# The gates of the last two token chunks by seven block products in place of eight, with sums made in PSUM banks

## The chip, the cores and the metric

The kernel runs on one core of one Trainium2 chip. The metric is the device time of one execution in microseconds. Five engines work side by side, each through its own instructions in order, and wait for each other by semaphores: TensorE (PE) multiplies matrices into PSUM, VectorE (DVE) and ScalarE (ACT) read PSUM and SBUF, GpSimd (POOL) works on SBUF, and SyncE (SP) issues most DMAs. PSUM has eight banks of 512 f32 columns here; SBUF is the working memory.

## The reference

```
phi(x) = elu(x) + 1                       # q, k, v: [8 batches, 8 heads, 576, 64]
kv = phi(k).T @ v ;  z = sum(phi(k))      # per batch and head
x  = (phi(q) @ kv) / (phi(q) . z + 1e-6)  # -> [4608 tokens, 512]
a  = x @ w1 ;  b = x @ w2                 # [4608, 1024] each
out = ((a * b) @ w3) @ w_out              # [4608, 512]
```

Inputs and output are f32. The two last products are one with the weight wf = w3 @ w_out.

## The kernel before

The 4608 tokens are 36 tiles of 128, and four tiles make one of nine chunks c0 of 512 columns. Attention gives x for three tiles at a time (NT makes numerators and denominators on PE, NM divides on VectorE), and a DMA transposes it (XD) into `xt` of a chunk: 512 features in four blocks of 128 rows, bf16.

The feed-forward part of a chunk has two kinds of steps. `F.c0.f` (f from 0 to 7) makes 128 of the 1024 hidden features for the chunk's 512 tokens: four matmuls for side a (`a_ps`), four for side b (`b_ps`), each into a PSUM bank of its own; ScalarE copies a to SBUF (L492), and VectorE multiplies the copy with b into the bf16 tile `ab` (L494). `O.t` makes the output of one tile t: eight matmuls with `wf_sb` into one bank (L536), a copy by ScalarE (.a) or VectorE (.v) (L543), and `S.t` stores it in two DMAs. `Q.35` is the last tile, in three pieces.

Other steps that the change moves: L (loads: LV is v), EX, PT and PM (phi of q or k: exp on ScalarE, two operations on VectorE), VC (v to bf16), KB (kv of a batch), QD (transposed q by DMA).

A table of text, `ORDER`, lists all steps; the program is emitted in that order, and each engine gets its instructions in it. PSUM is given out by hand: four single banks (kind "mm") and two tiles of two banks (kind "at"), first freed first taken. SBUF buffers of the loads (kind "ld", 13 of them) are handed out in the same way. A tile framework puts in the semaphore waits.

Of the kernel before, what the change touches and what calls it, by code (L numbers as in the profile page):

```python
# [19 lines left out]
T3.7.0.v LO.0 CO.0.a LO.2 CO.1.v FW.2.0.a T3.7.1.a LO.3 FW.4.0.a CO.3.a LQ.0.0 L3.6 FW.7.0.a
PT.q.0.0 L3.1 FW.2.1.a FW.4.1.a EX.q.0.0 LQ.0.1 PM.q.0.0 CO.2.p FW.2.2.a FW.7.1.a FW.7.2.v FW.7.3.a
FW.4.2.a FW.4.3.v QP.0.0.v C3.6.a LK.0.0 T3.1.0.a T3.1.1.a PT.q.0.1 FW.2.3.v L3.3 L3.5 T3.6.0.v
T3.6.1.v EX.q.0.1 LK.0.1 FW.1.0.a FW.1.1.a PT.k.0.0 FW.1.2.a PM.q.0.1 FW.6.0.a FW.6.1.v FW.6.2.v
LH.0.0 EX.k.0.0 T3.3.0.a T3.3.1.a FW.1.3.a C3.5.v T3.5.0.a FW.6.3.v EX.k.0.1 PT.k.0.1 LV.0.0 LV.0.1
LH.0.1 FW.3.0.a FW.3.1.v T3.5.1.a FW.3.2.v FW.3.3.v PM.k.0.1 LA.0 LB.6 I.2 CA.0.p CB.6.p LB.7
PM.k.0.0 T3.0.0.a LA.1 FW.5.0.a VC.0.0.a QP.0.1.v FW.0.0.a FW.0.1.a KV.0.0.a LA.2 VC.0.1.v FW.5.1.v
T3.0.1.v KV.0.1.a NT.0 NM.0.0 NM.0.1 CB.7.p FW.0.2.a FW.0.3.a NM.0.2 FW.5.2.a FW.5.3.a LA.3 XP.0.a  # L30
CA.2.p XP.1.v ND.3 LB.2 CA.1.v XP.2.a LB.3 FS.0.0.0.0 FS.0.1.0.0 FS.0.1.1.0 FS.0.0.1.0 LQ.1.1 LK.1.0
XP.3.v FS.0.2.0.0 FS.0.2.1.0 FS.0.2.0.1 FS.0.2.1.1 CB.2.v FS.0.0.0.1 FS.0.0.1.1 FS.0.1.0.1
FS.0.1.1.1 FS.0.3.0.1 CB.3.v PT.q.1.1 CA.3.p F.0.4 EX.q.1.1 PM.q.1.1 PT.k.1.0 LQ.1.0 LV.1.0 PT.q.1.0
EX.k.1.0 FS.0.3.0.0 LK.1.1 F.0.5 F.0.6 PM.k.1.0 VC.1.0.v EX.q.1.0 PM.q.1.0 QP.1.1.a EX.k.1.1
FS.0.3.1.0 PT.k.1.1 LV.1.1 F.0.7 KV.1.0.a LQ.2.1 LQ.3.1 VC.1.1.a QP.1.0.a O.0.a PM.k.1.1 KV.1.1.v
LV.2.0 FS.0.3.1.1 EX.q.3.1 NT.4 NM.4.0 NM.4.1 O.1.a NM.4.2 EX.q.2.1 PT.q.2.1 LK.2.0 XP.4.a ND.7
XP.5.a LK.2.1 EX.k.2.1 LK.3.1 O.2.a PT.q.3.1 PT.k.2.1 LV.3.0 XP.6.v XP.7.v LV.2.1 EX.k.2.0 PM.k.2.1
LV.3.1 O.3.a PT.k.2.0 LQ.2.0 S.0.s LQ.3.0 PM.k.2.0 PM.q.2.1 VC.2.0.v LV.4.1 F.1.0 F.1.1 PT.k.3.1
# [24 lines left out]

# [1 line left out]
def kernel(  # L65
# [473 lines left out]

    def s_O(t, e):  # L540
        o_ps = o_mm(t, slice(0, DM))
        o_sbs[t] = take("o_sb", None, [P, DM], F32, "o_sb")
        copy_of(e)(out=o_sbs[t], in_=o_ps)  # L543
        give("mm", "o_ps")

    def store(queues, t, o_sb, cols):
        for g in range(2):
            b, j = divmod(2 * t + g, J)
            queues[g].dma_start(out=out[b * S:(b + 1) * S, :].rearrange("(p j) n -> p j n", j=J)[:, j, cols],
                                in_=o_sb[g * R:(g + 1) * R, cols])  # L550
# [53 lines left out]
```

## Time and profile before

| | us |
|---|---|
| median of three runs | 240.89 (240.65 to 241.69) |
| span of the profiled execution, first to last instruction | 239.7 |
| PE busy | 233.2 |
| DVE busy | 151.0 |
| ACT busy | 115.0 |
| POOL busy | 8.1 |

The page gives the span of the profiled execution and no time of its own beside it. Busy times are sums over an engine's instructions; an engine that is busy for less than the span may still be waited for at some place. Rows of the timeline give the start, the duration, the engine, the line of the kernel, what is written and read, and in brackets the idle time before and what ended it. Matmuls overlap at their ends, so a row of four shows 1.03 us where the next four start 0.86 us later.

### The profile page before, as it was taken

How to read it: one execution, taken by the hardware profiler on the slowest of the kernel's cores; microseconds unless marked ns; L12 is line 12 of the kernel's file. 1: busy time of each engine (PE TensorE's matmuls, PEld its weight loads, DVE VectorE, ACT ScalarE, POOL GpSimd, SP SyncE). 2: the span in 40 equal slices, each digit the busy share in tenths (PEclk: the TensorE clock that was granted, in tenths of full speed). 3: DMA queues.
4: the chain of work that ended last, by engine and by line, in shares of the span. 5: the costliest groups of instructions: out<-in, count | busy, mean ns of one | idle time of the engine just before them, and what ended most of it. 6: DMA issues, size and time to landing. Idle time of an engine off the chain costs nothing.

```text
span 239.7 us, 5540 instructions
## 1 busy us (share of the span) xinstructions
PE 233.2 (97%) x2276; PEld 120.2 (50%) x2276; DVE 151.0 (63%) x278; ACT 115.0 (48%) x173; POOL 8.1 (3%) x15
## 2 busy tenths in 40 slices
PE   8899999999999999999999999999999999999994
PEld 5656668555445444444454444545444444444443
DVE  0347787889999646877862588885546363433341
ACT  2576743979793255568522656424232113321300
POOL 1020053000000000000000000000000000000000
PEclk9999999999999999999999999999999999999999
DMA  6999999999996999999879959965293763005216
GB/s 241 402 406 397 379 375 390 390 390 389 396 332 137 158 357 247 323 406 296 190 106 192 392 123 262 320 116 131 52 178 69 174 157 88 3 0 125 50 24 154
DMA packets 52553, 55.81 MB, mean 233 GB/s; under 512 B 31280, under 2 KB 32560, under 8 KB 52528
## 3 DMA queue, kind: packets, MB, share of 16 engines
q1 hardware_dynamic: 52288, 55.19, 78.5%
q8 instruction: 18, 0.29, 0.5%
q10 hardware_dynamic: 240, 0.26, 0.3%
q14 instruction: 7, 0.06, 0.1%
HBM read 38.80 MB, written 9.44 MB: 201 GB/s over the span
## 4 chain that ended last, share of the span: by engine, by line
PE 96%; DVE 1%; ACT 1%; issue 0%
PE o_ps L536 26%; PE a_ps L483 25%; PE b_ps L483 24%; PE wf_ps L264 6%; PE nd L399 3%; PE w3p L252 3%; PE warm L149 2%; PE kbp L341 2%; PE a_ps L516 2%; PE b_ps L516 2%; PE xp L458 1%; PE qp L369 1%; PE kvp L341 1%; ACT wo_sb L218 0%; ACT w3b L238 0%; DVE w3t L253 0%
## 5 line engine op out<-in xcount | busy, mean ns | idle before, releaser
L483 PEld LDWEIGHTS <-w_sb 128*128 128x128 bf16 x544 | 52.6, 98 | 62.5 <-DVE xt L459 0.3
L494 DVE TENSOR_TENSOR ab<-a_sb,b_ps 128x512 bf16<-128x512 f32 x68 | 46.2, 686 | 39.9 <-PE b_ps L483 38.6
L492 ACT COPY a_sb<-a_ps 128x512 f32<-128x512 f32 x68 | 39.8, 586 | 64.0 <-PE a_ps L483 63.6
L483 PE MATMUL a_ps<-xt,w_sb 128*128 128x512 bf16 x272 | 69.9, 380 | 0.0
L483 PE MATMUL b_ps<-xt,w_sb 128*128 128x512 bf16 x272 | 69.8, 379 | 0.0
L536 PE MATMUL o_ps<-wf_sb,ab 128*128 128x512 bf16 (+2 forms) x304 | 65.2, 368 | 0.0
L536 PEld LDWEIGHTS <-ab 128*128 128x128 bf16 x304 | 28.4, 98 | 31.7 <-issue 0.4
L543 ACT COPY o_sb<-o_ps 128x512 f32<-128x512 f32 x22 | 12.9, 586 | 33.5 <-PE o_ps L536 26.7
L405 DVE TENSOR_TENSOR xn<-nd,r 128x512 bf16<-128x512 f32 (+2 forms) x47 | 23.8, 559 | 0.3
L274 ACT ACTIVATE ek<-k 128x1152 bf16<-128x1152 f32 x16 | 18.7, 1172 | 0.7 <-ACT ek L274 0.7
L274 ACT ACTIVATE eq<-q 128x1152 bf16<-128x1152 f32 x16 | 18.7, 1168 | 0.4 <-DMA q<-in_q_dram 0.4
L543 DVE COPY o_sb<-o_ps 128x512 f32<-128x512 f32 x13 | 9.0, 691 | 15.3 <-PE o_ps L536 12.6
L264 PE MATMUL wf_ps<-wo_sb,w3t 128*128 128x512 bf16 x64 | 15.6, 380 | 0.5 <-ACT wo_sb L218 0.5
L286 DVE TENSOR_SCALAR phq<-q 128x1152 bf16<-128x1152 f32 x16 | 12.0, 755 | 2.7 <-DMA q<-in_q_dram 2.7
L294 DVE TENSOR_TENSOR phk<-phk,ek 128x1152 bf16<-128x1152 bf16 x16 | 11.9, 750 | 1.8 <-ACT ek L274 1.7
L294 DVE TENSOR_TENSOR phq<-phq,eq 128x1152 bf16<-128x1152 bf16 x16 | 12.1, 755 | 1.0 <-ACT eq L274 0.8
L286 DVE TENSOR_SCALAR phk<-k 128x1152 bf16<-128x1152 f32 x16 | 12.0, 753 | 0.0
L264 PEld LDWEIGHTS <-w3t 128*128 128x128 bf16 x64 | 5.9, 98 | 5.8 <-issue 0.7
L328 ACT CAST vt<-v 128x1152 bf16<-128x1152 f32 x7 | 8.1, 1162 | 0.9 <-DMA v<-in_v_dram 0.9
L253 ACT CAST w3t<-w3p 128x512 bf16<-128x512 f32 x7 | 4.0, 587 | 9.3 <-PE w3p L252 7.4
L399 PEld LDWEIGHTS <-qt 64*64 64x64 bf16 x576 | 6.1, 106 | 4.3 <-issue 4.1
L399 PE MATMUL nd<-kv,qt 64*64 64x65 bf16 x576 | 7.6, 194 | 0.4 <-DVE w3t L253 0.4
(57 smaller groups left out, 127.4 us busy)
## 6 DMA issues: line engine op xcount, KB each, us to landing
q<-in_q_dram SPq DMA_DIRECT2D x16, 576.0 KB, 8.3
k<-in_k_dram SPq DMA_DIRECT2D x16, 576.0 KB, 9.5
v<-in_v_dram SPq DMA_DIRECT2D x16, 576.0 KB, 10.5
out_dram<-o_sb SPq DMA_DIRECT2D x69, 128.0 KB, 2.5
w<-in_moe_w_dram SPq DMA_DIRECT2D x7, 512.0 KB, 10.9
wo<-in_moe_w_out_dram SPq DMA_DIRECT2D x4, 512.0 KB, 8.2
wa<-in_moe_w_dram SPq DMA_DIRECT2D x4, 512.0 KB, 10.7
wb<-in_moe_w_dram SPq DMA_DIRECT2D x4, 512.0 KB, 10.4
```

What stands on the lines that cost most here:

```text
L264: nc.tensor.matmul(wfs[i], w3ts[i][:, c, :], wo_sb[:, c, :], start=(c == 0), stop=(c == FC - 1))
L274: nc.scalar.activation(out=t, in_=raw[n, b, h], func=AF.Exp)
L286: (nc.gpsimd if e == "p" else nc.vector).tensor_scalar(out=by_set(n, t), in0=by_set("k", raw[n, b, h]), scalar1=0.0, scalar2=1.0, op0=ALU. ...
L294: nc.vector.tensor_tensor(out=t, in0=t, in1=by_set("k", es[n, b, h]), op=ALU.min)
L399: nc.tensor.matmul(dst[g * R:(g + 1) * R], qts[b, a // 2][rows, j, a % 2 * R:(a % 2 + 1) * R], kvs[b][rows, a // 2, a % 2, :], start=True, ...
L405: nc.vector.tensor_tensor(out=xn[:, :, a0:a1], in0=n4[:, :, :, 0:D], in1=r.unsqueeze(3).to_broadcast([P, 2, a1 - a0, D]), op=ALU.mult)
L483: nc.tensor.matmul(ops_[key][:, tiles.start * P:tiles.stop * P], w[:, w_row(kc), f * P:(f + 1) * P], xts[c0][:, tiles, kc, :], start=(kc = ...
L492: nc.scalar.copy(out=a_sbs[c0, f], in_=ops_[key])
L494: nc.vector.tensor_mul(out=abs_[c0][:, f, :], in0=a_sbs[c0, f], in1=ops_[key])
L516: nc.tensor.matmul(p, w[:, w_row(kc), f * P:(f + 1) * P], xts[c0][:, 2 * g:2 * g + 2, kc, :], start=(kc == 0), stop=(kc == KC - 1))
L536: nc.tensor.matmul(o_ps, abs_[c0][:, f, m * P:(m + 1) * P], wf_sb[:, f, cols], start=(f == 0), stop=(f == FC - 1))
L543: copy_of(e)(out=o_sbs[t], in_=o_ps)
```

## The change

For chunks 7 and 8 together, the gates are taken as a 2 by 2 block product: the hidden features in two halves, the 512 input features in two halves, the two chunks as two halves of the columns. Seven block products take the place of eight, for each of four values of f and each side (Winograd's form of Strassen's method). The weight sums (four for each side, step WS) are made on GpSimd, the sums of `xt` (four, step WT) on VectorE. A step `WP.7.f.side.i` makes product i in two matmuls of 512 columns, and takes the results apart in a row of sums: products 1, 6, 7, 4 build up in the first bank of an "at" tile, 5 and 3 in the second, 2 in an "mm" bank. ScalarE copies the bank after 1, 5 and 6 (and after 4 on side a); VectorE adds such a copy to the bank after 2, 7 and 3. On side b the sum is multiplied with side a's at once, in SBUF, into the bf16 tile `abq`.

```diff
+    def ws_of(side, i):
+        key = ("ws", side, (i - 1) // 2)
+        if key not in wsum:
+            wsum[key] = late(key, 4).rearrange("p (i r n) -> p i r n", i=2, r=2)
+        return wsum[key][:, (i - 1) % 2]
...
+    def s_WS(side, i, e):
+        w = (w1_sb, w2_sb)[side]
+        a, b, op = {1: (w_half(w, 0, 1), w_half(w, 1, 1), ALU.add),
+                    2: (ws_of(side, 1), w_half(w, 0, 0), ALU.subtract),
+                    3: (w_half(w, 0, 0), w_half(w, 0, 1), ALU.subtract),
+                    4: (w_half(w, 1, 0), ws_of(side, 2), ALU.subtract)}[i]
+        (nc.gpsimd if e == "p" else nc.vector).tensor_tensor(out=ws_of(side, i), in0=a, in1=b, op=op)
...
+    def w_mm(ps, c0, f, side, i, first):
...
+        for r in range(2):
+            nc.tensor.matmul(ps, lhs[:, r, f * P:(f + 1) * P], rhs[:, :, r, :],
+                             start=(first and r == 0), stop=(r == 1), skip_group_check=not first)
...
+    def w_add(c0, f, side, ps, tmp, c, g):
+
+        nc.vector.tensor_tensor(out=tmp, in0=ps, in1=tmp, op=ALU.add)
+        if side == 0:
+            wtmp[c0, f, "a", c, g] = tmp
+        else:
+            nc.vector.tensor_mul(out=w_ab(c0, f)[:, c, g], in0=wtmp.pop((c0, f, "a", c, g)), in1=tmp)
+
+    def s_WP(c0, f, side, i, e):
+        q = c0, f, side
+        if i in (1, 5) and q not in wbank:
+            wbank[q] = at_tile("wp" + "ab"[side], ("wp",) + q)
+        if i == 2:
+            wbank[q + ("x",)] = mm_tile("wx" + "ab"[side], ("wx",) + q)
+        ps = wbank[q + ("x",)] if i == 2 else wbank[q][:, 0 if i in (1, 6, 7, 4) else 1]
+        w_mm(ps, c0, f, side, i, i in (1, 2, 5))
+        if i in (1, 5, 6):
+            t = wtmp[q + (i,)] = w_tmp({1: "e", 5: "phq", 6: "phk"}[i], "p" + str(i) + "ab"[side])
+            nc.scalar.copy(out=t, in_=ps)
+        elif i == 2:
+            w_add(c0, f, side, ps, wtmp.pop(q + (1,)), 0, 0)
+            give("mm", ("wx",) + q)
+        elif i == 3:
+            w_add(c0, f, side, ps, wtmp.pop(q + (6,)), 1, 0)
+        elif i == 7:
+            w_add(c0, f, side, ps, wtmp.pop(q + (5,)), 1, 1)
+        elif side == 0:
+            t = wtmp[c0, f, "a", 0, 1] = w_tmp("w3t", "p4a")
+            nc.scalar.copy(out=t, in_=ps)
+        else:
+            nc.vector.tensor_mul(out=w_ab(c0, f)[:, 0, 1], in0=wtmp.pop((c0, f, "a", 0, 1)), in1=ps)
+        if i == 4:
+            give("at", ("wp",) + q)
```

The order is another one from the step behind `PM.q.6.1` on; ahead of it nothing is changed. A piece of the table as it was (all of F.7) and as it is:

```diff
-S.22.s S.23.s O.26.v O.27.v F.7.0 S.24.s XD.8.0 S.25.s F.7.1 F.7.2 F.7.3 F.7.4 F.7.5 F.7.6 XD.8.1
+WP.7.2.1.3 WP.7.2.1.4 O.27.a WP.7.3.0.5 S.26.s WP.7.3.0.1 S.20.s WP.7.3.0.2 WP.7.3.1.1 WP.7.3.1.2
```

Products and PE's other steps in their new order, a product written as f, side, number (0a1 is WP.7.0.0.1), and the first product some 22 us of PE work behind `PM.q.6.1`:

```
0a1 F.6.7 F.6.4 0b1 F.6.2 O.22 0a2 0a6 0a5 0b5 F.6.5 0a7 0a3 0b6 0b3 0a4 0b7 F.6.6 0b4
1a1 0b2 1a5 1a6 1b1 F.6.0 1a7 1b6 1a3 1b5 1a4 1b7 O.24 2b1 1b4 1b3 O.20
2a1 2b6 2b5 2a6 1a2 2a5 1b2 2a7 O.26 2b7 2a3 2a4 2a2 2b3 2b4 O.27
3a5 3a1 3a2 3b1 3b2 3a6 3b6 3b5 3a7 2b2 3b7 3a3 3a4 O.25 3b4 3b3
O.30 O.31 O.32 O.34 O.29 O.33 O.28 Q.35
```

The attention steps of the last batch (KB.7, NT.30, NT.33, QD.7, XD.7, XD.8) now all come ahead of 0a1.

Three places show how instructions stand on the engines. First TensorE, before, where one side's matmuls end and the next begin in an F step of chunk 8:

```order
L483 MATMUL b_ps<-xt,w_sb 128x512
L483 LDWEIGHTS w_sb
L483 MATMUL a_ps<-xt,w_sb 128x512 [waits Activation_49]
L483 LDWEIGHTS w_sb
L483 MATMUL a_ps<-xt,w_sb 128x512
```

TensorE in the changed kernel at 2a3, 2a4 and 2a2 (`wpa` is the tile of two banks of side a, `wxa` the single bank of product 2, `ws` and `xs` the sums):

```order
L632 LDWEIGHTS ws
L632 MATMUL wpa<-xt,ws 128x512 [waits DVE_49]
L632 LDWEIGHTS ws
L632 MATMUL wpa<-xt,ws 128x512
L632 LDWEIGHTS w_sb
L632 MATMUL wpa<-xs,w_sb 128x512 [waits DVE_49]
L632 LDWEIGHTS w_sb
L632 MATMUL wpa<-xs,w_sb 128x512
L632 LDWEIGHTS w_sb
L632 MATMUL wxa<-xt,w_sb 128x512
```

Before, a wait comes once in four matmuls and is for a bank used two steps earlier; now 2a4, into the first bank, waits for a VectorE instruction, and the count of its wait is that of the add behind 2a3, which reads the second bank. Second, VectorE, before, from the divisions of NT.33 to the multiplications of chunks 7 and 8:

```order
L405 TENSOR_TENSOR xn<-nd,r 128x512
L543 COPY o_sb<-o_ps 128x512 [waits DMAHW7_49,DMAHW0_49,PE_49]
L543 COPY o_sb<-o_ps 128x512 [waits DMAHW2_49,DMAHW1_49,PE_49]
L494 TENSOR_TENSOR ab<-a_sb,b_ps 128x512 [waits PE_49,Activation_49] x11
L543 COPY o_sb<-o_ps 128x512 [waits DMAHW4_49,DMAHW3_49,PE_49]
```

VectorE in the changed kernel, from the add behind 3a7 to the end of the products:

```order
L648 TENSOR_TENSOR p5a<-wpa,p5a 128x512 [waits PE_49]
L648 TENSOR_TENSOR p1b<-wxb,p1b 128x512 [waits PE_49]
L652 TENSOR_TENSOR abq<-p1a,p1b 128x512 [waits DVE_49]
L648 TENSOR_TENSOR p5b<-wpb,p5b 128x512 [waits PE_49,Activation_49]
L652 TENSOR_TENSOR abq<-p5a,p5b 128x512 [waits DVE_49]
L648 TENSOR_TENSOR p6a<-wpa,p6a 128x512 [waits PE_49]
L676 TENSOR_TENSOR abq<-p4a,wpb 128x512 [waits PE_49,Activation_49]
L648 TENSOR_TENSOR p6b<-wpb,p6b 128x512 [waits PE_49]
L652 TENSOR_TENSOR abq<-p6a,p6b 128x512 [waits DVE_49]
```

One multiplication for each F step has become a row of adds and multiplications, and the add behind 3a3 (`p6a`) stands fourth behind the add of 3a7 (`p5a`), after two adds and two multiplications for other products. Third, GpSimd, whose last instructions before were casts of weights in the front of the program:

```order
L227 CAST w_sb<-wb 128x2x512 [waits DMAHW4_49]
L227 CAST w_sb<-wb 128x2x512 [waits DMAHW5_49]
L222 CAST w_sb<-wa 128x2x512 [waits DMAHW7_49]
L222 CAST w_sb<-wa 128x2x512 [waits DMAHW0_49]
L599 UNCONDITIONAL_BRANCH
```

In the changed kernel, behind the same casts:

```order
L616 TENSOR_TENSOR ws<-w_sb 128x1024 [waits DMAHW1_49,DMAHW5_49,DVE_49,DMAHW6_49,Activation_49,Pool_49]
L616 TENSOR_TENSOR ws<-w_sb 128x1024 [waits DVE_49,DMAHW2_49,PE_49,DMAHW6_49,Activation_49,Pool_49]
L616 TENSOR_TENSOR ws<-ws,w_sb 128x1024 [waits Pool_49] x2
L616 TENSOR_TENSOR ws<-w_sb,ws 128x1024 [waits DMAHW2_49,DMAHW4_49,Activation_49,Pool_49]
L616 TENSOR_TENSOR ws<-w_sb,ws 128x1024 [waits DMAHW2_49,DMAHW7_49,DVE_49,Activation_49]
L616 TENSOR_TENSOR ws<-w_sb 128x1024 x2
```

Eight sums are added. They wait for the last readers of the load buffers that they write: VC.5.1 for the first, PT.k.7.0 for the second, VC.6.0 for the fifth and EX.k.7.1 for the sixth, all of them steps in the part that isn't changed.

More of the change, by code (lines that the diff above doesn't have):

```diff
@@ L16 @@
 NCH = 512
+PAIRS = (7,)
 ORDER = """
 L3.7 L3.4 L3.2 LO.1 I.0 H.1.1 H.3.0 H.1.2 I.1 T3.4.0.a H.2.3 T3.2.0.v T3.2.1.a T3.4.1.v H.1.4 C3.7.a
[L23 to L38, printed above, removed]
@@ L530, in s_FP, with ab_of @@
             f_out(c0, f, side)
+    def ab_of(c0, f):
+        if c0 in PAIRS:
+            return quads[c0, f % 4][:, 0, f // 4]
+        if c0 - 1 in PAIRS:
+            return quads[c0 - 1, f % 4][:, 1, f // 4]
+        return abs_[c0][:, f]
     def o_mm(t, cols):
@@ L535, in o_mm @@
         for f in range(FC):
-            nc.tensor.matmul(o_ps, abs_[c0][:, f, m * P:(m + 1) * P], wf_sb[:, f, cols],
+            nc.tensor.matmul(o_ps, ab_of(c0, f)[:, m * P:(m + 1) * P], wf_sb[:, f, cols],
                              start=(f == 0), stop=(f == FC - 1))
@@ L544, in s_O @@
         give("mm", "o_ps")
+        c0 = t // CT - (t // CT - 1 in PAIRS)
+        if c0 in PAIRS:
+            n = uses["o", c0] = uses.get(("o", c0), 0) + 1
+            if n == 2 * CT:
+                for f in range(FC // 2):
+                    give("ld", ("abq", c0, f))
     def store(queues, t, o_sb, cols):
@@ L563, in s_Q, with late, w_half, x_half @@
             store((nc.sync, nc.scalar), t, o_sb, slice(pieces[0][0], pieces[-1][1]))
+    quads, wsum, xsum, wbank, wtmp, uses = {}, {}, {}, {}, {}, {}
+    def late(key, n):
+        t = take("ld", key, [P, HW], F32, key[0]).bitcast(BF16)[:, 0:n * NCH]
+        return t
+    def w_half(w, k, fh):
+        return w[:, 2 * k:2 * k + 2, fh * NCH:(fh + 1) * NCH]
+    def x_half(c0, k):
+        return xts[c0][:, :, k::2, :]
+    def ws_of(side, i):
[3 more added lines that the diff above has]
+        return wsum[key][:, (i - 1) % 2]
@@ new lines, in xs_of @@
+    def xs_of(c0, i):
+        key = ("xs", c0, (i - 1) // 2)
+        if key not in xsum:
+            xsum[key] = late(key, 4).rearrange("p (i m r n) -> p i m r n", i=2, m=CT, r=2)
+        return xsum[key][:, (i - 1) % 2]
+    def s_WS(side, i, e):
[5 more added lines that the diff above has]
+        (nc.gpsimd if e == "p" else nc.vector).tensor_tensor(out=ws_of(side, i), in0=a, in1=b, op=op)
@@ new lines, in s_WT @@
+    def s_WT(c0, i, e):
+        b11, b12, b21, b22 = x_half(c0, 0), x_half(c0 + 1, 0), x_half(c0, 1), x_half(c0 + 1, 1)
+        a, b = {1: (b12, b11), 2: (b22, xs_of(c0, 1)), 3: (b22, b12), 4: (b21, xs_of(c0, 2))}[i]
+        (nc.gpsimd if e == "p" else nc.vector).tensor_tensor(out=xs_of(c0, i), in0=a, in1=b, op=ALU.subtract)
+    def w_mm(ps, c0, f, side, i, first):
+        w = (w1_sb, w2_sb)[side]
+        lhs = {1: lambda: w_half(w, 0, 0), 2: lambda: w_half(w, 1, 0), 3: lambda: ws_of(side, 4),
+               4: lambda: w_half(w, 1, 1), 5: lambda: ws_of(side, 1), 6: lambda: ws_of(side, 2),
+               7: lambda: ws_of(side, 3)}[i]()
+        rhs = {1: lambda: x_half(c0, 0), 2: lambda: x_half(c0, 1), 3: lambda: x_half(c0 + 1, 1),
+               4: lambda: xs_of(c0, 4), 5: lambda: xs_of(c0, 1), 6: lambda: xs_of(c0, 2),
+               7: lambda: xs_of(c0, 3)}[i]()
+        for r in range(2):
+            nc.tensor.matmul(ps, lhs[:, r, f * P:(f + 1) * P], rhs[:, :, r, :],
+                             start=(first and r == 0), stop=(r == 1), skip_group_check=not first)
@@ new lines, in w_tmp, with w_ab @@
+    def w_tmp(kind, name):
+        t = take(kind, None, [P, FC, P] if kind == "w3t" else [P, HW], BF16, name)
+        if kind == "w3t":
+            t = t.rearrange("p c t -> p (c t)")
+        return t.bitcast(F32)[:, 0:NCH]
+    def w_ab(c0, f):
+        if (c0, f) not in quads:
+            quads[c0, f] = late(("abq", c0, f), 4).rearrange("p (c g n) -> p c g n", c=2, g=2)
+        return quads[c0, f]
+    def w_add(c0, f, side, ps, tmp, c, g):
[4 more added lines that the diff above has]
+            nc.vector.tensor_mul(out=w_ab(c0, f)[:, c, g], in0=wtmp.pop((c0, f, "a", c, g)), in1=tmp)
@@ new lines, in s_WP @@
+    def s_WP(c0, f, side, i, e):
[23 more added lines that the diff above has]
+            give("at", ("wp",) + q)
+        if i > 3:
+            n = uses[c0, i in (4, 7)] = uses.get((c0, i in (4, 7)), 0) + 1
+            if n == 4 * FC // 2:
+                give("ld", ("xs", c0, int(i in (4, 7))))
+        if i in (3, 5, 6, 7):
+            n = uses["s", side, i in (3, 7)] = uses.get(("s", side, i in (3, 7)), 0) + 1
+            if n == FC * len(PAIRS):
+                give("ld", ("ws", side, int(i in (3, 7))))
```

63 lines of the change are left out of this document (42 added, 21 removed).

## Prediction

> **What bounds the kernel now.** I read the shares of the page first, then the chain that ended last, then a table by stretches of time, then the rows of the last chunks one by one.
>
> ```profile
> span 239.7 us, 5540 instructions
> PE 96%; DVE 1%; ACT 1%; issue 0%
> ```
>
> ```profile
> core 0: us, PE busy (x) PEld busy (x) DVE busy (x) ACT busy (x) POOL busy (x), PEclk, DMA share, GB/s
> 0.00:20.00 20.00, 17.42 (x90) 11.74 (x91) 6.86 (x11) 10.12 (x13) 2.72 (x10) 1.00 0.92 355
> 150.93:173.50 22.57, 22.57 (x334) 11.29 (x332) 15.88 (x32) 8.31 (x13) 0.00 (x0) 1.00 0.65 142
> 173.50:218.50 45.00, 45.00 (x301) 20.55 (x300) 21.51 (x39) 11.79 (x21) 0.00 (x0) 1.00 0.44 96
> ```
>
> TensorE (PE) holds 96% of the chain, and in the stretches that the change rewrites (the last two rows) it is busy for all of the time at a granted clock of 1.00, while VectorE (DVE) and ScalarE (ACT) are less than three quarters busy. So a matmul taken out here shortens the kernel by its full slot, as long as nothing new makes PE wait. The slot comes from the chain in order of time:
>
> ```profile
> 227.47 0.86 PE a_ps L483 x4
> 228.33 0.86 PE b_ps L483 x4
> ```
>
> Four 128x512 matmuls hold the chain for 0.864 us (228.33 less 227.47 is 0.86), so one is 0.216 us and a product of two matmuls 0.43 us.
>
> **What is removed.** Chunks 7 and 8 took 16 steps of 8 matmuls, 128 in all. Now they take 4 output blocks f, 2 sides, 7 products, 2 matmuls each: 112. That is 16 x 0.216 = **3.5 us less** on PE.
>
> **What is added on PE: waits.** A product is called f, side, number here: 2a4 is product 4 of side a in block f = 2. The products of one f and side share one PSUM tile of two banks (only number 2 has a bank of its own). By design 1, 6, 7, 4 build up in the first bank and 5, 3 in the second, and the order of products makes use of that: 7 and 3, or 6 and 5, often follow each other directly. But the waits in the built program are by the tile and not by the bank: the first matmul of 2a4 waits for VectorE's read of 2a3, and the wait count it names is that of the add issued just for 2a3, although that add reads the other bank. So PE has to stand through a whole read. What a read takes, from a matmul's last slot to the next start:
>
> ```profile
> 225.58 1.03 PE L483 MATMUL a_ps<-xt,w_sb 128*128 128x512 bf16 x4
> 226.44 1.03 PE L483 MATMUL b_ps<-xt,w_sb 128*128 128x512 bf16 x4
> 226.65 0.58 ACT L492 COPY a_sb<-a_ps 128x512 f32<-128x512 f32 x1 [1.14 <-PE a_ps L483]
> 227.31 1.03 PE L483 MATMUL a_ps<-xt,w_sb 128*128 128x512 bf16 x4
> 227.58 0.69 DVE L494 TENSOR_TENSOR ab<-a_sb,b_ps 128x512 bf16<-128x512 f32 x1 [1.04 <-PE b_ps L483]
> ...
> 10.57 1.05 ACT L218 CAST wo_sb<-wo 128x1024 bf16<-128x1024 f32 x1
> 11.67 0.59 PE L264 MATMUL wf_ps<-wo_sb,w3t 128*128 128x512 bf16 x2 [0.54 <-ACT wo_sb L218]
> ```
>
> The a group's slots end at 226.44, and ScalarE starts at 226.65: 0.21 us for the end of the pipeline and the semaphore. Its copy takes 0.58. PE starts 0.05 us after the engine it waits for (11.67 less 11.62). So a wait on ScalarE costs 0.21 + 0.58 + 0.05 = **0.84 us**, less what PE has to do in between. VectorE starts 0.27 after the slots (227.58 less 227.31) and takes 0.69: **1.01 us**. The adds themselves (PSUM plus an SBUF tile, f32) are not in the trace; L494, with the same operands and a bf16 result, is the nearest row; bounds are the 0.42 us of the same operation at half the width and the 0.755 of a product of two SBUF tiles of over twice the width:
>
> ```profile
> L494 DVE TENSOR_TENSOR ab<-a_sb,b_ps 128x512 bf16<-128x512 f32 x68 | 46.2, 686 | 39.9 <-PE b_ps L483 38.6 <-ACT a_sb L492 0.8 <-issue 0.3
> L294 DVE TENSOR_TENSOR phq<-phq,eq 128x1152 bf16<-128x1152 bf16 x16 | 12.1, 755 | 1.0 <-ACT eq L274 0.8
> L523 DVE TENSOR_TENSOR ab<-a_sb,b_ps 128x256 bf16<-128x256 f32 x8 | 3.3, 420 | 1.6 <-PE b_ps L516 1.5
> ```
>
> I take 0.69 for sums and multiplications.
>
> Going down the order of products, 19 of them stand directly behind a read of their own tile, or one or two products behind it, and these are all the waits that are not covered:
> - ScalarE, nothing in between: 0a5, 0b3, 1a6, 2b5, 3a1, 3b5: 6 x 0.84 = 5.0
> - ScalarE, one product (0.43) in between: 1a5, 2a5, 2a7: 3 x 0.41 = 1.2
> - VectorE, nothing in between: 0a3, 1b3, 2a4, 2b4, 3a4, 3b3: 6 x 1.01 = 6.1
> - VectorE, one in between: 0b7, 1a3, 1a4: 3 x 0.58 = 1.7; two in between: 3a3, 0.15
>
> That makes 18 waits with a cost and one of 0.15, **14.2 us**. All others have an F or O step of 1.73 us, or two products, ahead of them and cost nothing.
>
> Where VectorE has a queue, the wait is longer, since it works in order. Two operations back to back take 1.28 us, so one behind another starts 0.60 later; a product of two sums has to wait for the second sum, and starts 0.03 after its end, as here (182.12, then 182.15):
>
> ```profile
> 140.37 1.28 DVE L494 TENSOR_TENSOR ab<-a_sb,b_ps 128x512 bf16<-128x512 f32 x2
> ...
> 181.95 0.17 DVE L432 TENSOR_SCALAR r<-nd 128x10 f32<-128x10 f32 x1
> 182.15 0.30 DVE L433 RECIPROCAL r<-r 128x24 f32<-128x24 f32 x1
> ```
>
> The worst is 3a4. Count from the end of 3a7's slots: VectorE adds for 3a7 at 0.27 to 0.96, for 2b2 at 0.88 to 1.57, multiplies at 1.60 to 2.29, adds for 3b7 at 2.21 to 2.90, multiplies at 2.93 to 3.62, and only then adds for 3a3, at 3.54 to 4.23. PE could have begun 3a4 at 1.44 and begins at 4.28: 2.84 in place of 1.01, **1.8 more**. In the same way 2a4 waits 1.91 (the add of 2b7 and a multiplication stand ahead): 0.9 more. 0a3, 1a3 and 2b4 find one operation ahead and lose 0.2 each, and four copies on ScalarE 0.05 to 0.08 each: 0.8 together. **The waits come to 14.2 + 3.5 = 17.7 us**, in a stage that holds 208 matmuls (112 of the products, 48 of six F steps, 48 of six O steps), 45 us of PE work.
>
> VectorE as a whole isn't the bound: 40 operations for 16, six F and two O steps and four sums of xt come to 52 x 0.69 = 36 us in a stage that is 45 us of PE work alone. ScalarE makes 28 copies for 16, 12 x 0.58 = 7 us more, with three quarters of the stretch idle now (11.79 of 45).
>
> **What is moved, and other new work.** Batch 7's divisions (NT.30, NT.33) come some 16 to 20 us sooner. Behind them VectorE has 10 us of work in the 11.7 us between F.5.2 and NT.27 and about as much up to the first product; the transposes XD of chunks 7 and 8 are issued about as their divisions end, and F.6.7 and F.6.4 (3.5 us) cover the sums that wait for them. I take 0; it would cost up to 0.8 if that cover falls short.
>
> The eight weight sums on GpSimd (POOL) wait only for buffers long free, so they start far ahead of their place in the order: the last four at 135.6, when ScalarE has cast a v tile, and run in a row.
>
> ```profile
> 33.17 1.04 POOL L227 CAST w_sb<-wb 128x1024 bf16<-128x1024 f32 x1 [0.34 <-DMA wb<-in_moe_w_dram]
> 35.59 0.68 DVE L222 CAST w_sb<-wa 128x1024 bf16<-128x1024 f32 x1
> 35.99 1.18 POOL L222 CAST w_sb<-wa 128x1024 bf16<-128x1024 f32 x1 [1.78 <-DMA wa<-in_moe_w_dram]
> ...
> 134.43 1.16 ACT L328 CAST vt<-v 128x1152 bf16<-128x1152 f32 x1
> 137.22 0.75 DVE L286 TENSOR_SCALAR phk<-k 128x1152 bf16<-128x1152 f32 x1
> 141.27 1.03 PE L483 MATMUL b_ps<-xt,w_sb 128*128 128x512 bf16 x4
> ```
>
> A GpSimd cast of 128x1024 takes 1.04 us alone and 1.18 when it starts under a VectorE cast. A sum reads two operands, so my estimate from these rows is 1.04 to 2.1 us. Nobody waits for the sums (the first product that needs one is 40 us later); the cost can only be VectorE held up by them. Its slack there: the product at 140.37 ends at 140.97 and frees the bank that PE writes from 141.27, so 0.3 us. Bounds 0 and 7 us (below); I take 0.4, nearest to the 0.14 that the row at 35.99 shows.
>
> At the end, the store of O.28 now stands ahead of the last tile's on the SP queue:
>
> ```profile
> 177.27 2.48 SPq L549 DMA_DIRECT2D out_dram<-o_sb  x4
> ```
>
> An issue is 0.62 us. Four of them (O.33, O.28) now stand between the last whole tiles and the last tile's own, where three did (O.33 and half of O.34); half of the added one lies beside the last copy: 0.3, between 0 and 0.62.
>
> **The sum.** -3.5 + 17.7 + 0.4 + 0.3 = +14.9 us. Against the profiled span: 239.7 + 14.9 = 254.6. The median of the runs, 240.89, lies 1.2 above that span, for what lies around it, so **255.8 us**, 6% slower.
>
> **The rivals.**
> *Faster: the waits do not bind.* If PE is held only by the read of the bank it writes, successive products of a bank are at least 0.86 us apart, which covers the 0.84, and what is left is 0.3 or so: 240.89 - 3.5 + 0.3 + 0.3 = 238.0. It decides once the 19 waits together cost under 3.5 us, 0.18 each. For it speaks that every order of products was laid out that way; against it, the waits in the program. The Trainium skill, "PSUM — Partial Sum Buffer", summary of rules, asks only that a bank be guarded while it is read and that a running matmul target another; by that rule the result would be this one. No run so far shows the two banks of one tile in use at once. 8%.
>
> *Slower still: GpSimd holds VectorE.* If VectorE stands until all four sums are through, its operation at 137.22 waits until 135.6 + 4 x 1.04 to 2.1 = 139.8 to 144.0, 2.6 to 6.8 late, and PE, with 0.3 in hand, loses 2.3 to 6.5: 257.7 to 261.9. It decides from one sum that delays VectorE by over 0.3. The Trainium skill, "SBUF — State Buffer", "Who interferes with whom", says that the later of two such operations blocks fully until the first is done; the 1.18 against 1.04 agrees for one direction. 12%.
>
> *The clock drops.* PE stops some 19 times, for 0.4 to 2.8 us. At half the clock the 45 us of PE work would double, while the waits, with more beside them, would lose some 6 us: 295. The Trainium skill, "TensorE: Matmul & The Clock Gate", on the second failure mode, "psum-queue depth-cycling", says that micro-idles between groups can do this. Against it: in the first 20 us PE idles 2.6 us and the clock stays at 1.00. 2%.
>
> **How the numbers follow.** My forecast has 78%, the rivals 8, 12 and 2. The low end is the waits without any queue on VectorE and nothing from GpSimd: 240.89 - 3.5 + 14.2 = 251.6. The high end takes in the lower half of the second rival, 260. Under 0.5% (1.2 us) is about what a measurement cannot tell from no change. Faster 7% (the first rival but for a part of it), the same 1%, slower 92%.
>
> **What would show it.** In the profile after: idle time on PE in front of L632, put down to DVE L648 and L676 and to ACT L664, near 18 us in 19 pieces, the longest ahead of 3a4; none of it in front of F and O steps. If PE has no gaps between directly following products of one tile, the first rival holds. GpSimd sums near 136 to 145 with longer VectorE rows of L292 and L300 would show the second, PEclk under 1.00 the third. Wrong I would be above all if VectorE's sums were much off 0.69 us, since a quarter of them stand in the way of PE.

## The result, and the profile after

| | before | after |
|---|---|---|
| median of four runs, us | 240.93 (240.65 to 241.69) | 259.85 (257.07 to 260.9) |
| span of the profiled execution | 239.7 | 258.1 (this run took 260.08) |
| ratio of times, with 95% interval | | 1.0751 [1.0689, 1.0813] |

The changed kernel is 7.5% slower, 4 us above the forecast and just inside the range.

The page of the changed kernel, its span, the busy times and the chain that ended last by engine:

```profile
span 258.1 us, 5560 instructions
...
PE 234.6 (91%) x2260; PEld 118.8 (46%) x2260; DVE 167.8 (65%) x301; ACT 124.3 (48%) x190; POOL 26.4 (10%) x23
...
PE 78%; DVE 8%; DMA 5%; ACT 4%; issue 2%; SPq 1%; DVEq 0%; ACTq 0%
```

PE's share of the chain fell from 96% to 78%. VectorE, ScalarE and DMAs now stand in the chain, though VectorE is busy for 65% of the span and ScalarE for 48%. Where this happens is told by the waits of PE by what was waited for (total, times, longest), for the changed kernel:

```profile
PE wpa L632 <- DVE p6a L648: 4.7, 3, 2.7
PE wpb L632 <- ACT p6b L664: 2.1, 3, 0.7
PE wpb L632 <- DVE abq L676: 1.7, 2, 0.8
PE wpa L632 <- ACT p5a L664: 1.6, 3, 0.7
PE wpa L632 <- DVE p5a L648: 1.6, 2, 1.0
PE wpb L632 <- DVE p6b L648: 1.4, 2, 0.9
PE b_ps L489 <- ACT o_sb L556: 1.3, 1, 1.3
...
PE b_ps L489 <- DVE ab L500: 0.5, 1, 0.5
```

All but the last two rows stand before L632, the products, and were put there by the three readers of their tiles (L648, L664, L676). The rows of the timeline show them one by one; here five of the eighteen, PE in the changed kernel, with the idle time ahead in brackets:

```profile
190.00 0.59 PE L632 MATMUL wpa<-xt,ws 128*128 128x512 bf16 x2 [1.02 <-DVE p5a L648]
...
196.99 0.59 PE L632 MATMUL wpa<-xs,ws 128*128 128x512 bf16 x2 [0.24 <-ACT p1a L664]
198.26 0.59 PE L632 MATMUL wpa<-xs,ws 128*128 128x512 bf16 x2 [0.67 <-ACT p5a L664]
...
220.08 0.59 PE L632 MATMUL wpa<-xs,w_sb 128*128 128x512 bf16 x2 [1.68 <-DVE p6a L648]
...
231.25 0.59 PE L632 MATMUL wpa<-xt,ws 128*128 128x512 bf16 x2
234.50 0.59 PE L632 MATMUL wpa<-xs,w_sb 128*128 128x512 bf16 x2 [2.66 <-DVE p6a L648]
234.93 3.46 PE L549 MATMUL o_ps<-wf_sb,ab 128*128 128x512 bf16 x8
238.19 0.75 PE L632 MATMUL wpb<-xs,w_sb 128*128 128x512 bf16 x2
```

A row of two matmuls shows 0.59 us where it holds 0.43 of slots, so each bracket is 0.16 short of the time lost. For 3a4 the rows give it directly: the slots of 3a3 end at 231.25 + 0.43 = 231.68, 3a4 starts at 234.50, and 2.82 us are lost. The 18 brackets make 14.35 us; with 18 x 0.16 = 2.88, and 0.08 at 3a3, the waits cost **17.3 us**.

The last two rows show something else: the eight matmuls of O.25 take 3.46 us, where such a row takes 1.89 (218.50 in e1, below), and the next product 0.75 for 0.59. By stretches of 1 us (length, then busy time of PE, PEld, DVE, ACT, POOL, then the granted clock), for the changed kernel:

```profile
234.00:235.00 1.00, 0.50 (x3) 0.26 (x3) 0.45 (x1) 0.00 (x0) 0.00 (x0) 1.00 0.00 0
235.00:236.00 1.00, 1.00 (x4) 0.33 (x3) 0.00 (x0) 0.59 (x1) 0.00 (x0) 0.54 0.00 0
236.00:237.00 1.00, 1.00 (x4) 0.40 (x3) 0.00 (x0) 0.00 (x0) 0.00 (x0) 0.50 0.00 0
237.00:238.00 1.00, 1.00 (x4) 0.36 (x3) 0.00 (x0) 0.00 (x0) 0.00 (x0) 0.50 0.00 0
238.00:239.00 1.00, 0.94 (x3) 0.25 (x2) 0.00 (x0) 0.57 (x1) 0.00 (x0) 0.75 0.00 0
```

The clock falls to 0.50 right behind the longest gap and is back some 3.4 us later. That costs 1.57 + 0.16 = 1.7 us.

The stage from 0a1 to O.30 ran from 176.33 to 240.22, 63.9 us for 44.9 us of work (208 x 0.216): 19.0 lost, 17.3 by waits and 1.7 by the clock. The rest of the difference lies ahead of the stage, in these rows of PE in the changed kernel; before the change PE had no idle row from 112 to 148 or from 150 to 176 us:

```profile
141.77 1.02 PE L489 MATMUL b_ps<-xt,w_sb 128*128 128x512 bf16 x4 [0.53 <-DVE ab L500]
161.86 1.02 PE L489 MATMUL b_ps<-xt,w_sb 128*128 128x512 bf16 x4 [1.29 <-ACT o_sb L556]
...
167.54 1.03 PE L405 MATMUL nd<-kv,qt 64*64 64x65 bf16 x48
...
172.05 0.58 PE L405 MATMUL nd<-kv,qt 64*64 64x65 bf16 x48
172.88 1.02 PE L489 MATMUL a_ps<-xt,w_sb 128*128 128x512 bf16 x4 [0.25 <-DMA xt<-xn]
```

With 0.16 for the tail, 0.7 us are lost at 141.77, 1.45 at 161.86 and 0.4 at 172.88. NT.30, at 167.54, takes 0.45 us longer than NT.33 at 172.05 with no wait shown.

### The profile page after: what moved, and what is told of

The parts are those of the page before. It is cut to its first block, busy times and chain, and to the rows that moved or that the text cites. A ratio compares the mean times of both kernels' runs of the same rounds, so it can differ in the third digit from the quotient of the medians.

```text
span 258.1 us, 5560 instructions
## 1 busy us (share of the span) xinstructions
PE 234.6 (91%) x2260; PEld 118.8 (46%) x2260; DVE 167.8 (65%) x301; ACT 124.3 (48%) x190; POOL 26.4 (10%) x23
## 4 chain that ended last, share of the span: by engine, by line
PE 78%; DVE 8%; DMA 5%; ACT 4%; issue 2%; SPq 1%; DVEq 0%; ACTq 0%
PE o_ps L549 23%; PE b_ps L489 16%; PE a_ps L489 16%; PE wf_ps L270 6%; PE wpa L632 4%; PE wpb L632 3%; DMA w<-in_moe_w_dram 2%; PE w3p L258 2%; DMA xt<-xn 2%; PE nd L405 2%; PE a_ps L522 1%; PE b_ps L522 1%; PE kbp L347 1%; DVE xn L411 1%; DVE ab L500 1%
## 5 line engine op out<-in xcount | busy, mean ns | idle before, releaser
L489 PEld LDWEIGHTS <-w_sb 128*128 128x128 bf16 x416 | 40.2, 98 | 49.8 <-issue 2.7
L489 PE MATMUL b_ps<-xt,w_sb 128*128 128x512 bf16 x208 | 53.4, 379 | 1.8 <-ACT o_sb L556 1.3
L489 PE MATMUL a_ps<-xt,w_sb 128*128 128x512 bf16 x208 | 53.4, 379 | 0.2 <-DMA xt<-xn 0.2
L500 DVE TENSOR_TENSOR ab<-a_sb,b_ps 128x512 bf16<-128x512 f32 x52 | 35.3, 685 | 27.7 <-PE b_ps L489 24.9
L549 PE MATMUL o_ps<-wf_sb,ab 128*128 128x512 bf16 x224 | 53.1, 388 | 0.0
L498 ACT COPY a_sb<-a_ps 128x512 f32<-128x512 f32 x52 | 30.4, 587 | 33.0 <-PE a_ps L489 32.6
L549 PEld LDWEIGHTS <-ab 128*128 128x128 bf16 x224 | 21.6, 99 | 25.4 <-issue 1.5
L411 DVE TENSOR_TENSOR xn<-nd,r 128x512 bf16<-128x512 f32 (+2 forms) x47 | 23.9, 559 | 0.4
L616 POOL TENSOR_TENSOR ws<-w_sb 128x1024 bf16<-128x1024 bf16 x4 | 8.8, 2200 | 78.9 <-DVE vt L334 76.8
L632 PEld LDWEIGHTS <-ws 128*128 128x128 bf16 x64 | 6.2, 97 | 17.9 <-issue 12.1
L549 PE MATMUL o_ps<-wf_sb,abq 128*128 128x512 bf16 (+2 forms) x80 | 14.0, 336 | 0.0
L632 PEld LDWEIGHTS <-w_sb 128*128 128x128 bf16 x48 | 4.8, 99 | 13.2 <-issue 8.3
L549 PEld LDWEIGHTS <-abq 128*128 128x128 bf16 x80 | 7.2, 98 | 6.9
```

The source lines that it names most:

```text
L411: nc.vector.tensor_tensor(out=xn[:, :, a0:a1], in0=n4[:, :, :, 0:D], in1=r.unsqueeze(3).to_broadcast([P, 2, a1 - a0, D]), op=ALU.mult)
L489: nc.tensor.matmul(ops_[key][:, tiles.start * P:tiles.stop * P], w[:, w_row(kc), f * P:(f + 1) * P], xts[c0][:, tiles, kc, :], start=(kc = ...
L498: nc.scalar.copy(out=a_sbs[c0, f], in_=ops_[key])
L500: nc.vector.tensor_mul(out=abs_[c0][:, f, :], in0=a_sbs[c0, f], in1=ops_[key])
L549: nc.tensor.matmul(o_ps, ab_of(c0, f)[:, m * P:(m + 1) * P], wf_sb[:, f, cols], start=(f == 0), stop=(f == FC - 1))
L616: (nc.gpsimd if e == "p" else nc.vector).tensor_tensor(out=ws_of(side, i), in0=a, in1=b, op=op)
```

## Experiments

Each ran beside the kernel before on the same chip: e1 to e4 together (before 241.18 us, 20 runs), e5 to e8 together on another chip (before 241.18, 17 runs).

### e1: a bank of its own for each sum

The theory: PE waits because the two banks of a product pair are one tile, and the framework's wait is for the last reader of the tile. The rival: what PE waits for is the read of the very bank it writes, or the queue of VectorE, and would stay.

```diff
+    def w_pair(q, name):
+        if "wb" not in pools:
+            ps_at.__exit__(None, None, None)
+            pools["wb"] = ctx.enter_context(tc.tile_pool(name="pswb", bufs=1, space=bass.MemoryType.PSUM))
+        s = slots[("wp",) + q] = free["at"].popleft()
+        return [pools["wb"].tile([P, NCH], F32, tag=f"wb{s}{k}", name=name) for k in range(2)]
...
-            wbank[q] = at_tile("wp" + "ab"[side], ("wp",) + q)
+            wbank[q] = w_pair(q, "wp" + "ab"[side])
...
-        ps = wbank[q + ("x",)] if i == 2 else wbank[q][:, 0 if i in (1, 6, 7, 4) else 1]
+        ps = wbank[q + ("x",)] if i == 2 else wbank[q][0 if i in (1, 6, 7, 4) else 1]
```

> The changed kernel with the same order, but each bank of a product pair is a PSUM tile of its own, so a product waits only for the last read of its own bank. If the waits by the tile are the cause, the 17.3 us that PE lost between the first product and O.30 fall to 1.5 or less and the clock does not drop: 260 - 17.3 - 1.7 + 1.5 gives 241 to 243 us. If the stage is long because VectorE or ScalarE can't keep up with the adds and copies, the time stays above 252 us and PE waits in the same places. If the clock drop carries most of it, some 257 us.

Measured: 240.23 us (239.97 to 240.82), ratio to before 0.996 [0.9947, 0.9974], a little below the 241 to 243 expected: none of the 1.5 us allowed for waits that stay is needed. The order of the steps is that of the changed kernel, the same operations run on the same engines, and 19.6 us are gone. The stage from 0a1 to O.30, in the same columns as above, and at 3a3, 3a4 and O.25 (lines are two further on), in e1:

```profile
176.21:221.09 44.88, 44.72 (x205) 20.37 (x209) 32.38 (x51) 20.99 (x38) 0.00 (x0) 1.00 0.24 55
```

```profile
217.64 0.59 PE L634 MATMUL wpa<-xt,ws 128*128 128x512 bf16 x2
218.07 0.59 PE L634 MATMUL wpa<-xs,w_sb 128*128 128x512 bf16 x2
218.50 1.89 PE L551 MATMUL o_ps<-wf_sb,ab 128*128 128x512 bf16 x8
...
220.24 0.68 DVE L650 TENSOR_TENSOR p6a<-wpa,p6a 128x512 f32<-128x512 f32 x1
```

44.88 us for 208 matmuls is 0.2158 each: no wait and no clock drop is left. 3a4 starts 0.43 us behind 3a3, and VectorE adds for 3a3 only at 220.24, 2.2 us after 3a4 began. Its queue is as long as before; PE just doesn't stand behind it any more. That is the theory; the rival falls.

The Trainium skill, "PSUM — Partial Sum Buffer", section "PSUM bank collisions raise a hardware error", asks for semaphores by bank; e1's waits are of that kind. What coarser ones cost is shown here: by the bank the stage takes 44.9 us, by a tile of two banks 63.9.

### e2 and e3: the stalls ahead of the stage

e2 takes e1 and moves one step, the store S.14. In the changed kernel the trace shows this chain (SP's queue and ScalarE):

```profile
152.96 4.99 SPq L392 DMA_TRANSPOSE qt<-phq  x2
157.99 1.31 SPq L568 DMA_DIRECT2D out_dram<-o_sb  x2
...
161.23 0.59 ACT L556 COPY o_sb<-o_ps 128x512 f32<-128x512 f32 x1 [3.28 <-DMA out_dram<-o_sb]
161.71 1.08 ACT L498 COPY a_sb<-a_ps 128x512 f32<-128x512 f32 x2
```

S.14 stands behind two transposes (QD.6) that hold the queue for 5 us, so its buffer is free only at 161.2; ScalarE's copy of O.19 waits for that buffer, the a copies of F steps queue behind it, and PE's `b_ps` at 161.86 waits in its turn.

```diff
-... LV.7.0 F.5.6 LV.7.1 WS.1.1.p
-S.16.s S.17.s PM.q.6.0 NT.24 QD.6.1 WS.0.1.p QD.6.0 VC.7.0.a S.14.s WS.1.2.p
+... LV.7.0 F.5.6 LV.7.1 WS.1.1.p S.14.s
+S.16.s S.17.s PM.q.6.0 NT.24 QD.6.1 WS.0.1.p QD.6.0 VC.7.0.a WS.1.2.p
```

> As e1, and the store S.14 is put back ahead of the transposes QD.6.1 and QD.6.0 on the SP queue, where it was before. If the 1.45 us at 161.9 (ScalarE held in O.19 by the buffer of O.14) and the two stalls of 0.4 us behind it (NT.30, F.6.1) all hang on that store, this is 2.0 to 2.3 us faster than e1, 239 to 241. If the later two come from the last batch's divisions being moved forward, only 1.4 us.

Measured: 239.9 us (239.28 to 240.28), ratio 0.9941 [0.9918, 0.9963]. The stall is gone from the trace, so its cause was the store. Its size was missed: the medians differ by 0.33 us, the spans of the profiled runs by 1.2 (239.0 and 237.8, e1's being the slowest of its ten runs). I had taken the size from the changed kernel; in e1's own trace the stall is 0.67 + 0.16 = 0.83 us. What the moved store is worth is settled only to between 0.3 and 1.2. Two waits are left between 100 and 225 us in e2:

```profile
141.71 1.02 PE L491 MATMUL b_ps<-xt,w_sb 128*128 128x512 bf16 x4 [0.53 <-DVE ab L502]
175.04 0.59 PE L634 MATMUL wpa<-xt,w_sb 128*128 128x512 bf16 x2 [0.43 <-DMA xt<-xn]
```

e3 then puts all eight weight sums ahead of LV.7.0 in the order, so that they run in one row from 114 to 133 us.

```diff
-... PM.q.6.1 LV.7.0 F.5.6 LV.7.1 S.14.s
+... PM.q.6.1 WS.1.1.p WS.0.1.p WS.1.2.p WS.0.2.p WS.0.4.p WS.1.4.p WS.1.3.p WS.0.3.p LV.7.0 F.5.6 LV.7.1 S.14.s
```

> As e2, and the eight sums on GpSimd take buffers that are free sooner, so that they run from about 114 to 133 us, where VectorE has idle time, and not at 135 to 145. If the 0.7 us at 141.8 is VectorE held up by a sum, it goes and no stall takes its place: 0.5 to 0.7 us faster than e2. If the sums hold VectorE up in the same way at 114 to 122 and PE waits for that, same as e2 or slower.

Measured: 241.0 us (240.78 to 242.33), ratio 0.9997 [0.998, 1.0014], 1.1 us more than e2. The stall at 141.7 is gone, but two others stand in its place, in e3:

```profile
117.75 0.78 PE L349 MATMUL kbp<-vt,phk 64*64 64x65 bf16 x71 [1.21 <-DVE ab L502]
129.56 1.02 PE L491 MATMUL a_ps<-xt,w_sb 128*128 128x512 bf16 x4 [1.03 <-DMA xt<-xn]
```

The first follows a VectorE operation held by a sum, as its second condition said: the product of two SBUF tiles at 114.43 (L302) takes 2.68 us there, and 0.75 with no sum. A place that suits the sums was not found by moving them all; e5 below tries the gap of VectorE's work.

### e4: is it the gap that drops the clock?

e4 is the changed kernel, waits and all, with four matmuls of zeros into a free bank between 3a3 and 3a4. The theory: the clock falls because PE stood still for so long. The rival: it falls for another reason, the many short stops before, and would fall here too.

```diff
-... WP.7.3.1.7 WP.7.3.0.3 WP.7.3.0.4 S.27.s O.25.a
+... WP.7.3.1.7 WP.7.3.0.3 H.4.9 WP.7.3.0.4 S.27.s O.25.a
```

> The changed kernel with four idle matmuls of zeros (f32, 128x256, 0.57 us each) between 3a3 and 3a4, where PE stood for 2.7 us. They write a bank that nobody reads. If the drop to half the clock for some 3 us behind that gap comes from PE standing idle, it goes: the granted clock is 1.00 in every run and the time 257 us, as in the one run of the changed kernel with a clock of 1.00, with no gap of over 1 us left there. If the drop comes from the many short stops, it stays: 259 to 260 us and a clock of 0.993.

Measured: 258.19 us (257.68 to 258.52), ratio 1.0704 [1.0676, 1.0731], 1.7 us less than the changed kernel though it does more. The two intervals overlap, so what decides is the trace. In e4 (the zeros are the eight rows of L155):

```profile
231.22 0.59 PE L632 MATMUL wpa<-xt,ws 128*128 128x512 bf16 x2
231.65 1.89 PE L155 MATMUL warm<-zero 128*128 128x256 f32 x8
234.48 0.59 PE L632 MATMUL wpa<-xs,w_sb 128*128 128x512 bf16 x2 [0.94 <-DVE p6a L648]
234.91 1.89 PE L549 MATMUL o_ps<-wf_sb,ab 128*128 128x512 bf16 x8
```

3a4 starts where it did (234.48 and 234.50), so the wait is whole, but O.25 takes 1.89 instead of 3.46. The mean clocks of the four runs are 0.998 to 1.000, against 0.993 in three of the four runs of the changed kernel; its fourth run, at 1.000, is the one of 257.07 us. (That is 2.6 us or more below the other three, where the drop accounts for 1.7; the rest was not followed up.) In e4's trace the 0.998 comes from a drop at 255.73, after the last matmul. So the long gap drops the clock here, in most runs and not in all; the other 17 stops, of 0.24 to 1.68, do not.

The traces narrow down when. In all ten, the recorded changes of the granted clock lie whole multiples of 3.413 us apart (in the changed kernel at 6.39, 235.08 and 238.50 us, 67 steps and one). In the step ahead of the drop PE was busy for 0.75 us, in the one that holds the stop of 1.68 us for 1.73. In the changed kernel, by these steps (columns as above):

```profile
218.02:221.43 3.41, 1.73 (x8) 0.68 (x7) 2.26 (x4) 0.73 (x2) 0.00 (x0) 1.00 0.58 133
231.67:235.08 3.41, 0.75 (x4) 0.29 (x3) 2.71 (x5) 0.00 (x0) 0.00 (x0) 1.00 0.00 0
235.08:238.50 3.42, 3.42 (x10) 1.22 (x8) 0.00 (x0) 0.66 (x2) 0.00 (x0) 0.50 0.00 0
```

The idle ends of the programs fit: in e2 the clock fell behind a step with 1.19 us of PE work (232.75 to 236.17), in e5 it held behind one with 1.43 (231.75 to 235.16). So how busy PE is in such a step seems to decide, and where the steps fall on a stop would then matter too. That this spared the fourth run is not shown, since it has no trace.

### e5, e6 and e7: what is left

e5 takes e2 and hands out the four buffers of the sums (a step WA) ahead of the loads of v of batch 7, so that no sum waits for the exp of batch 7's k.

```diff
+    def s_WA(e):
+        for side, i in ((0, 3), (1, 3), (1, 1), (0, 1)):
+            ws_of(side, i)
...
-... PM.q.6.1 LV.7.0 F.5.6
+... PM.q.6.1 WA LV.7.0 F.5.6
```

> As e2 (single banks, S.14 moved), with the four buffers of the weight sums taken ahead of the loads of v of batch 7, so that no sum has to wait for the exp of k of batch 7 (EX.k.7.1): all eight sums should run between 115 and 136 us, the last four in a stretch where VectorE is mostly idle. If the 0.7 us lost ahead of F.4.7's b at 141.7 come from sums that hold VectorE, this stall goes and nothing replaces it: 239.2, or 0.7 less than e2. Rival: VectorE is late there for another reason, or the later loads of v cost what the sums give back: the same as e2, 239.9, with a stall at 141.7 or a new one behind VC.7.0.

e6 is e5 with two more moves, and e7 is e2 with the same two:

```diff
-... S.18.s WP.7.0.0.1 S.23.s F.6.7 WT.7.1.v
+... S.18.s S.23.s F.6.7 WP.7.0.0.1 WT.7.1.v
...
-... S.33.s S.28.s Q.35
+... S.33.s S.28.b Q.35
```

> As e5, with F.6.7 ahead of product 0a1 (its 1.73 us cover the wait for the transpose XD.7, 0.6 us lost at 175.0 in e2) and the last whole tile's store (S.28) on two queues, one DMA each. If both stalls are what the trace shows, 0.6 + 0.3 less than e5: 238.3. Rival: F.6.7 is then missing as cover for the sums of xt (WT), and the stall moves to the second product: as e5, or 0.3 less for the store alone.

> As e2 (sums of weights where they were), with F.6.7 ahead of 0a1 and S.28 on two queues as in e6. By the trace 0.6 + 0.3 less than e2: 239.0, with the stall at 141.7 still there (0.7). The difference from e6 is the price of where the sums run. Rival: the same as e2, 239.9.

| | median, us | ratio to before |
|---|---|---|
| e2 | 239.9 | 0.9941 [0.9918, 0.9963] |
| e5: e2, sums in VectorE's gap | 238.84 (238.48 to 239.49) | 0.9906 [0.9888, 0.9924] |
| e7: e2, F.6.7 and S.28 moved | 239.05 (237.79 to 239.14) | 0.9903 [0.9882, 0.9924] |
| e6: both | 238.11 (237.6 to 239.82) | 0.9886 [0.9858, 0.9913] |

Each came within 0.4 us of what was expected. The sums, run earlier, bring 1.06 (e2 to e5) and 0.94 (e7 to e6); the trace had said 0.7. (e2 ran on the other chip; the medians of before are the same 241.18 on both.) The two moves bring 0.85 and 0.73; it had said 0.9. The intervals of e5, e6 and e7 overlap, so their order among themselves rests on the traces: e7 keeps only the stall at 142.0, e5 only those for `xt` (0.28 and 0.44), and e6 has no idle row on PE at all between 100 and 225 us. Its page:

```profile
span 236.1 us, 5544 instructions
...
PE 95%; DVE 1%; ACT 1%; issue 1%
```

e6 beats both kernels: 1.1% faster than before. By medians it is 3.07 us, of the 3.46 that 16 matmuls are worth.

### e8: the weight sums alone

e8 is the kernel before with the eight sums added and unused, placed behind LV.7.1 in the order.

> The kernel before with the eight weight sums on GpSimd added and nobody reading them (the gates stay as they were, so the sums are work that is left unused). If a GpSimd sum holds VectorE once, for what is left of the sum, one stall ahead of F.4.7's b near 141.3 and 0.7 us more than the kernel before: 241.6. My prediction took 0.4 for it: 241.3. If VectorE stood until a whole row of sums is through: 2.3 to 6.5 more, 243 or above. If the stall in the changed kernel came from its moved steps and not from the sums: no difference from before.

Measured: 241.79 us (241.39 to 242.49), ratio 1.0029 [1.0015, 1.0043], 0.6 more than before. VectorE, GpSimd and PE around the stall, in e8:

```profile
134.90 5.10 POOL L586 TENSOR_TENSOR ws<-w_sb,ws 128x1024 bf16<-128x1024 bf16 x2 [8.94 <-issue]
...
136.39 1.63 DVE L286 TENSOR_SCALAR phk<-k 128x1152 bf16<-128x1152 f32 x1
...
140.41 1.27 DVE L494 TENSOR_TENSOR ab<-a_sb,b_ps 128x512 bf16<-128x512 f32 x2
...
141.14 1.02 PE L483 MATMUL b_ps<-xt,w_sb 128*128 128x512 bf16 x4 [0.53 <-DVE ab L494]
```

The same places in e5, where the sums run some 8 us sooner:

```profile
126.36 4.20 POOL L622 TENSOR_TENSOR ws<-w_sb,ws 128x1024 bf16<-128x1024 bf16 x2
130.51 4.22 POOL L622 TENSOR_TENSOR ws<-w_sb 128x1024 bf16<-128x1024 bf16 x2
...
136.68 0.75 DVE L294 TENSOR_SCALAR phk<-k 128x1152 bf16<-128x1152 f32 x1
...
139.83 1.27 DVE L502 TENSOR_TENSOR ab<-a_sb,b_ps 128x512 bf16<-128x512 f32 x2
```

One VectorE operation takes 1.63 us under a sum and 0.75 without: it waits for what is left of one sum (the first of the two ends at 137.40), and the wait lies inside its recorded time. The delay reaches `ab` 4 us later and PE behind it. Without any part of the products the same stall stands there, so it comes from the sums and not from the moved steps.

## Why the prediction was right, and where its sizes were off

The differences by term, from the profiled executions (of the 0.5 us between the two sums, 0.2 is a front that ran ahead of before's; the rest was not followed up):

| term of the sum, us | forecast | measured |
|---|---|---|
| 16 matmuls less | -3.5 | -3.5 (0.2158 each in e1) |
| waits in the products | 17.7 | 17.3 |
| weight sums on GpSimd | 0.4 | 0.7 (e8 alone: 0.6) |
| moved steps | 0 (bound 0.8) | 2.3 |
| store at the end | 0.3 | 0.4 (last matmul's end to the span's end 3.91, before 3.52; in e7 3.39) |
| clock | 0 (a rival) | 1.7 |
| sum | +14.9 | +18.9 (spans: +18.4) |

**The waits were right, in place and in size.** PE stood at the 19 places that were named. By kinds, with the queue's share added to the forecast:

| | places | forecast | measured |
|---|---|---|---|
| ScalarE, nothing between | 6 | 5.3 | 5.2 |
| ScalarE, one product between | 3 | 1.2 | 1.3 |
| VectorE, nothing between | 6 | 9.2 | 9.0 |
| VectorE, one or two between | 4 | 2.0 | 1.9 |

The two long ones, 3a4 and 2a4, came to 2.82 and 1.84 us against 2.84 and 1.91. An f32 add of a bank and an SBUF tile, which no trace had shown, took what was taken for it: L648 shows 686 to 690 ns. That the waits go by the tile was read from the built program; e1 shows it on the chip.

**The first rival (the waits do not bind)** is what e1 makes true. It gave 240.2 and not the rival's 238.0: the rival's sum had the same gap as mine, nothing for the moved steps, and nothing for the weight sums either. e6, where those stalls and the late store are taken out, is at 238.1.

**The moved steps were mis-sized: 2.3 us for 0.** "I take 0" rested on VectorE's work and on F.6.7 and F.6.4 as cover for the sums of `xt`. Its bound of 0.8 named only that cover. What came late were other transposes, those of chunk 6: 0.4 us in front of F.6.1. What was left out is SP's queue: the store S.14 had come to stand behind the two QD.6, and through a buffer and two copies on ScalarE that reached PE, 1.45 us. e2 shows this cause. The wait for transposes moves about: it stands in front of F.6.1 in the changed kernel, of 0a1 in e1, e2 and e4 (0.40 to 0.43 us, chunk 7's), and of both in e5; e6 and e7, with F.6.7 ahead of 0a1, have neither, but no run was made for the one in front of F.6.1. The 0.45 us in NT.30 stay open: e6's NT.30 has 0.95 where NT.33 has 0.58. The trace has NT.30's weight loads wait 0.42 us for VectorE's divisions (L411); no run was made for it.

**GpSimd was nearly right, by luck in the size and for half of the right reason.** The 0.4 did not follow from the rows beside it: 0.14 of delay with 0.3 in hand would have cost nothing. The sums stood where they were forecast (135.5), but took 2.1 to 2.6 us each, at and above the upper end of my estimate of 1.04 to 2.1. The second rival's condition (one sum that delays VectorE by over 0.3) was met with 0.87, and its price was not: VectorE gets in after one sum, not after all four, so 0.7 and not 2.3 to 6.5 (0.87 less the 0.3 in hand is 0.6, what e8 shows). The Trainium skill, "SBUF — State Buffer", section "Who interferes with whom", says that the later operation blocks until the first one is done; 1.63 against 0.75 us in e8 agrees, for one operation at a time.

**The third rival (the clock drops) came about in small.** I gave it the whole stage or nothing; it took 3.4 us of it, behind one gap. The count of stops was the wrong thing to look at; the long one did it, and e4 shows that. My argument against the drop misread the first 20 us as well: the view gives 1.00, but before has no clock record ahead of 7.13 us, and there matmuls of zeros start 0.43 us apart (ten in 4.63 us, from 1.18), where e4's of the same shape start 0.22 apart (eight in 1.89 us). PE ran at half speed there. The Trainium skill, "TensorE: Matmul & The Clock Gate", section "A second HAM failure mode: psum-queue depth-cycling", lets many micro-idles between groups do this; here 17 of them did nothing to the clock.

The 4 us between forecast and result are these: 2.3 for the moved steps, 1.7 for the clock, 0.3 for GpSimd, 0.1 for the store, less 0.4 for the waits. That 259.85 lies inside a range that ends at 260 is luck: its upper part was kept for GpSimd, and two terms that stood at 0 filled it.

## What to carry to other kernels

Where partial sums in PSUM are read while the next product of the group builds up, look at what the built program waits for: with two banks in one tile, a plan that alternates banks gained nothing: its waits cost 17.3 us and the clock drop 1.7, against 3.5 us of matmuls saved. An order that is made anew has to be followed through the DMA queues as well, since a store that moves behind a slow transpose can come back, through a buffer and ScalarE, as a stall on PE. Work for GpSimd is best started where VectorE has a gap, and not only where its result is not yet needed.

## What was not expected of the hardware

- The clock fell to 0.50 for 3.4 us behind a stop of 2.66 us (in the 3.41 us before the drop PE was busy for 0.75); the mean clocks put it in three runs of four. Stops up to 1.68 us didn't do it, and the same stop cut to 0.94 us by matmuls of zeros didn't either. The Trainium skill, "TensorE: Matmul & The Clock Gate", section "HAM oscillation — how this bites in real kernels", puts the bound at some 3.4 us of idle time; here less was enough. Counted in steps of 3.41 us, every step with up to 1.19 us of PE work that ends in one of the ten traces is followed by the drop, and none with 1.43 or more is.
- VectorE's TENSOR_SCALAR from f32 in SBUF waits for a GpSimd sum inside its own recorded time (0.75 becomes 1.63 in e8), and so does its product of two SBUF tiles (0.75 becomes 2.68 in e3), so that the trace shows a busy engine and no wait. The multiplications that read PSUM kept their time (1.27 us for two in e8, under a sum, and in e5, with none).
